# Two units of P times V leave PSUM in one operation; halves out of place move by transfer; a new list of operations

## The chip, the cores and the metric

The kernel runs on one core of a Trainium2 chip. Its time is the device time of one launch in microseconds (us). TensorE (PE) multiplies matrices into PSUM; VectorE (DVE), ScalarE (ACT) and GpSimd (POOL) work element by element; SyncE (SP) and ACT issue transfers, which run on DMA engines beside the rest. Each engine runs its own instructions in the order in which they stand in the program and waits on semaphores for the others.

## The reference, cut to what matters

```
scores = scale * matmul(q, k^T), masked where the clusters of q and k differ     # 4 batches x 8 heads, 768 x 768, head size 64
attn   = exp(scores - max); attn = attn / (sum + 1e-9)
x      = matmul(attn, v), heads side by side                                   # 3072 tokens x 512
h      = x @ w_in;  g = h * tanh(softplus(h))                                  # 512 -> 2048
out    = g @ w_out                                                             # 2048 -> 512
```

## The kernel before

**Units.** The 32 heads (batch b, head h) are cut into three blocks qb of 256 queries: 96 units, in the list `units` in the order head by head, qb 0 1 2. A unit has two halves a of 128 queries. For each half `scores` puts 128 x 768 products into a PSUM buffer of the ring S, which has two buffers; `rowmax` (DVE) takes the row's maximum m, `expo` (ACT) writes p = exp(s - m) to SBUF and the sum l, and with that the buffer of S is free for the scores after next. `total`, `recip`, `p_hi` (POOL) and `p_lo` (DVE) make two fp16 parts hl of the scaled p, and `ptrans` (SP) turns them over by a transposing transfer into pt. The first 24 units (batch 0, the wide ones) keep f32 p and turn it over on PE instead (tiles q, then copies to pt).

**P times V.** `pv(m)` takes the units 2m and 2m+1 together: the first one's product lands on rows 0 to 63 of one PSUM tile o, the second one's on rows 64 to 127, 256 columns each. There is one buffer for o. Unit by unit, `pv_out` (ACT) then writes the high fp16 part of 64 rows to x, and `x_lo` (DVE) the low part as a difference. x is the transposed input of the feed-forward layer, one tile of 128 rows for each pair of heads c = h // 2 and each block qb: even heads own its rows 0 to 63, odd heads its rows 64 to 127, so rows are moved across partitions by these two operations. In the wide units ACT spreads 1/l as rb, DVE multiplies 64 rows a unit into xf, and the odd head's turn ends in one ACT copy and one POOL subtraction of 128 rows.

**Feed-forward.** For batch b and block tt, `m1` multiplies w_in by the four x tiles of tt into the tile h (ring of two), `e_mish` (ACT) applies the activation, `e_gh` (POOL) and `e_gl` (DVE) split it, `m2` multiplies by w_out into O, `m_out` and `m_store` write the rows out. ACT has to load a table each time it goes from exp to Mish and back. The feed-forward of a batch runs among the attention units of the next, and the last 512 tokens use a scheme with fewer products (`n_mul`, `k_mul`) at the end.

**What sets the order.** `ORDER` is a list of operation names written out by hand; `Plan` issues them in its order (an operation that needs another through `pl.after` pulls it forward), and `tie` keeps each engine, and each ring of buffers, in just this order. SP takes 144 transposing transfers and the loads, copies and stores, one after another.

Of the kernel before, what the change touches and what calls it, by code (L numbers as in the profile page):

```python
# [92 lines left out]
def tile_clustered_attention_mish_ffn(  # L93
# [698 lines left out]

    def pv_out(i):
        pl.after(("pv", i // 2, 2), *((("pv_out", i - 1),) if i % 2 else ()))
        g, qb, _ = units[i]
# [8 lines left out]
        if mode(i, 0) != 3:
            nc.scalar.activation(x[r2 : r2 + D, 0], o[:, :256], AF.Copy, scale=1.0 / PS)
            return
        if h % 2 == 0:
            st["xf", h // 2, qb] = hlp.tile([P, 256], F32, tag="hl", name=f"xf{h // 2}_{qb}")
        xf = st["xf", h // 2, qb]
        if i % 2 == 0:  # L810
            st["rb"] = mp.tile([P, 256], F32, tag="osb", name=f"rb{i}", bufs=1)
            nc.scalar.activation(st["rb"], st["o", i // 2][:, 256:], AF.Copy, scale=vst[b, "p"])
        nc.vector.tensor_tensor(xf[r2 : r2 + D], o[:, :256], st["rb"][r : r + D], op=ALU.mult)
        if h % 2:
            nc.scalar.copy(x[:, 0], xf)
            nc.gpsimd.tensor_tensor(x[:, 1], xf, x[:, 0], op=ALU.subtract)

    def x_lo(i):
        pl.after(("pv_out", i))
# [6 lines left out]
        nc.vector.scalar_tensor_tensor(
            x[:, 1], o[:, :256], 1.0 / PS, x[:, 0], op0=ALU.mult, op1=ALU.subtract  # L830
        )
# [732 lines left out]
qk_load 1, qk_load 0, qk_load 2, qk_load 3, v_load 0 3, v_load 0 1, w_load 1, v_load 0 0, w_load 3, v_load 0 2,  # L1564
put_consts, centroids, prep_hi 1, prep_hi 0, prep_lo 0, cent_put, copy_t 1, copy_t 0, v_sq 0 3, copy_a 0, copy_z 0,
prep_lo 1, v_sq 0 1, copy_a 1, w_abs 1, v_sq 0 0, copy_b 0, w_load 2, w_load 0, w_load 16, w_load 7, w_load 4, w_load
17, w_load 6, w_load 11, w_load 5, w_load 10, assign_mm 0, assign_turn 0, assign_max 0, assign_hot 0, assign_back 0,
assign_put 0, hot_direct 1, hot_direct 0, w_abs 3, v_sq 0 2, assign_stg 0, hot_copy 0, scores 0 0, w_low 2, w_low 3,
w_low 1, scores 0 1, rowmax 0 0, rowmax 0 1, w_f32 3, copy_z 1, w_abs 2, hot_copy 1, expo 0 0, expo 0 1, w_abs 0, p_hi
0 1, w_low 0, p_hi 0 0, scores 1 0, p_lo 0 0, scores 1 1, p_lo 0 1, scores 2 0, rowmax 1 0, w_f32 2, v_max 0, rowmax 1  # L1570
1, w_f32 1, w_f32 0, rowmax 2 0, ptrans 0 0, expo 1 0, ptrans 0 1, expo 1 1, p_hi 1 1, p_hi 1 0, p_lo 1 0, scores 2 1,
v_cross 0, p_lo 1 1, ptrans 1 0, copy_b 1, rowmax 2 1, v_peak 0, ptrans 1 1, expo 2 0, w_low 7, prep_hi 2, w_low 6,
prep_lo 2, total 0 1, w_low 17, total 1 1, w_low 5, w_low 4, p_hi 2 0, w_abs 7, expo 2 1, p_hi 2 1, w_sq 0, pv 0 0,
p_lo 2 0, scores 3 0, v_wide 0, scores 3 1, pv 0 1, w_f32 7, recip 0 1, rowmax 3 0, recip 1 1, rowmax 3 1, copy_t 2,
w_load 9, w_load 8, copy_z 2, qk_load 4, hot_copy 2, copy_a 2, w_load 15, copy_b 2, w_load 12, pv 0 2, p_lo 2 1,
scores 4 0, ptrans 2 0, w_abs 5, w_abs 6, w_abs 4, expo 3 0, expo 3 1, ptrans 2 1, p_hi 3 1, p_hi 3 0, p_lo 3 0,
scores 4 1, w_sq 1, p_lo 3 1, scores 5 0, w_f32 6, w_f32 4, v_scale 0, rowmax 4 0, pv_out 0, pv_out 1, rowmax 4 1,
x_lo 0, x_lo 1, ptrans 3 0, expo 4 0, ptrans 3 1, expo 4 1, p_hi 4 1, p_hi 4 0, w_sq 2, p_lo 4 0, w_low 8, w_low 16,
total 3 1, total 4 1, total 2 1, prep_hi 3, prep_lo 3, w_low 9, recip 3 1, rowmax 5 0, recip 4 1, recip 2 1, w_f32 5,
total 1 0, w_abs 8, ptrans 4 0, w_abs 9, expo 5 0, total 0 0, recip 0 0, recip 1 0, scores 5 1, p_lo 4 1, pv 1 0, pv 1  # L1580
1, p_hi 5 0, pv 1 2, w_sq 3, p_lo 5 0, scores 6 0, w_f32 8, rowmax 5 1, ptrans 4 1, w_abs 17, w_f32 17, expo 5 1,
pv_out 2, p_hi 5 1, total 5 1, w_abs 12, recip 5 1, w_abs 16, ptrans 5 0, w_low 12, w_low 10, pv_out 3, w_low 15,
rowmax 6 0, expo 6 0, x_lo 3, scores 6 1, w_sq 4, w_sq 5, w_sq 6, w_sq 7, p_lo 5 1, scores 7 1, w_f32 9, rowmax 6 1,
ptrans 5 1, w_f32 12, rowmax 7 1, expo 6 1, x_lo 2, p_hi 6 1, p_hi 6 0, p_lo 6 0, scores 7 0, pv 2 0, qk_load 5,
qk_load 7, w_load 14, w_load 13, w_load 21, qk_load 6, copy_z 3, copy_t 3, hot_copy 3, w_load 20, copy_b 3, copy_a 3,
w_load 18, w_load 22, w_load 19, v_load 1 0, total 3 0, rowmax 7 0, w_abs 11, w_abs 10, w_abs 14, w_abs 15, w_abs 13,
expo 7 0, ptrans 6 0, expo 7 1, p_hi 7 1, recip 3 0, total 4 0, recip 4 0, total 2 0, recip 2 0, pv 2 1, pv 2 2, w_low
11, w_low 14, w_low 13, total 6 1, total 7 1, w_f32 11, w_f32 14, recip 6 1, w_f32 10, w_f32 13, w_f32 15, w_f32 16,
w_low 21, pv_out 4, p_hi 7 0, assign_mm 1, p_lo 6 1, scores 8 0, w_sq 8, w_sq 9, p_lo 7 0, scores 8 1, w_sq 10, w_sq
11, w_sq 12, p_lo 7 1, w_sq 13, w_sq 14, total 5 0, x_lo 4, assign_turn 1, rowmax 8 0, assign_max 1, recip 7 1, rowmax  # L1590
8 1, ptrans 6 1, w_abs 21, ptrans 7 0, expo 8 0, prep_hi 4, w_f32 21, ptrans 7 1, w_sq 15, expo 8 1, total 8 1, pv_out
5, w_sum 0, p_hi 8 0, p_lo 8 0, scores 9 0, w_spread 0, pv 3 0, p_hi 8 1, assign_hot 1, rowmax 9 0, assign_back 1, pv
3 1, pv 3 2, assign_put 1, scores 9 1, recip 5 0, w_scale 0, recip 8 1, assign_stg 1, rowmax 9 1, w_abs 20, ptrans 8
0, expo 9 0, w_abs 18, pv_out 6, pv_out 7, x_lo 6, x_lo 7, p_hi 9 0, p_lo 8 1, scores 10 0, w_sq 16, p_lo 9 0, ptrans
8 1, expo 9 1, ptrans 9 0, w_low 20, w_low 22, prep_lo 4, w_low 19, w_low 18, w_hi 0, p_hi 9 1, w_f32 18, rowmax 10 0,
w_lo 0, scores 10 1, p_lo 9 1, ptrans 9 1, rowmax 10 1, expo 10 0, expo 10 1, w_abs 19, total 6 0, recip 6 0, w_sq 17,
pv 4 0, total 9 1, w_hi 1, recip 9 1, w_f32 20, w_lo 1, p_hi 10 1, p_hi 10 0, p_lo 10 0, scores 11 0, pv 4 1, pv 4 2,
copy_t 4, copy_a 4, copy_z 4, hot_copy 4, w_load 25, copy_b 4, w_load 26, w_load 23, total 9 0, recip 9 0, scores 11
# [315 lines left out]
```

## Time and profile before

| | us |
|---|---|
| three timed runs | 857.17, 860.67, 860.91 (median 860.67) |
| profiled execution | 856.9, of which the span 855.2 |
| PE busy | 833.8 |
| DVE busy | 675.7 |
| ACT busy | 544.1 |
| POOL busy | 433.6 |

The span runs from the first instruction to the last. Busy shares are averages over stages: up to about 188 us the wide units run, to about 735 us the other units and the feed-forward, then the feed-forward of the last batch alone. Idle time of an engine matters where it is the engine that ends last.

### The profile page before, as it was taken

Reading aid. Unit: us, or ns where it says so; the run is one execution under the profiler, and the core shown is the slowest. Engines: PE = TensorE matmul, PEld = TensorE weight load, DVE = VectorE, ACT = ScalarE, POOL = GpSimd, SP = SyncE. Lnnn points to the kernel's source line nnn. Section 1 sums busy time; section 2 is a strip of 40 time slices with the busy share of each in tenths; the row PEclk is TensorE's granted clock in tenths of the full one; section 3 lists DMA queues with packets and bytes.
Section 4 is the critical chain, followed back from the end, with each engine's and each line's share of the span. In section 5 each row is a group of like instructions: output and inputs, shape, how many; then the busy total and the mean of one; then the engine's idle time right before and its main releaser. Section 6 shows DMA issues by size and latency. Waiting matters only on the chain.

```text
span 855.2 us, 17553 instructions
## 1 busy us (share of the span) xinstructions
PE 833.8 (97%) x6743; PEld 622.9 (73%) x6743; DVE 675.7 (79%) x1192; ACT 544.1 (64%) x925; POOL 433.6 (51%) x417
## 2 busy tenths in 40 slices
PE   8999999999999999999999999999999999999998
PEld 3777776776777677676777766776777776688887
DVE  7899988998788787777878786788878776898822
ACT  7987976775678564676567566576675663455600
POOL 2567865876666465664565356555648433110000
PEclk9999999999999999999999999999999999999999
DMA  9986751798998996986988987888878754000002
GB/s 339 298 247 185 213 135 43 114 192 163 176 200 154 174 181 122 148 163 116 173 153 174 190 171 127 150 177 162 136 146 146 148 112 96 15 1 2 2 8 80
DMA packets 253460, 122.50 MB, mean 143 GB/s; under 512 B 230368, under 2 KB 230880, under 8 KB 253376
## 3 DMA queue, kind: packets, MB, share of 16 engines
q1 hardware_dynamic: 249216, 112.30, 62.7%
q10 hardware_dynamic: 4160, 9.08, 5.3%
q8 instruction: 53, 0.87, 0.4%
q14 instruction: 31, 0.25, 0.1%
HBM read 35.72 MB, written 6.29 MB: 49 GB/s over the span
## 4 chain that ended last, share of the span: by engine, by line
PE 52%; DVE 4%; DMA 3%; ACT 2%; POOL 1%; issue 1%; ACTq 0%; SPq 0%; POOLq 0%; DVEq 0%
PE h L847 7%; PE h L849 6%; PE h L848 6%; PE o L768 5%; PE O L984 5%; PE O L985 5%; PE O L986 5%; PE s L646 3%; PE s L651 3%; DMA pt<-hl 2%; PE cn L937 2%; DVE hl L732 1%; PE cy('k', 1)_10960 L1131 1%; PE cy('k', 0)_10720 L1131 1%; DVE m L663 1%
## 5 line engine op out<-in xcount | busy, mean ns | idle before, releaser
L677 ACT ACTIVATE p<-s,m 128x768 f32<-128x768 f32 x192 | 173.0, 902 | 120.4 <-DVE m L663 59.1
L715 POOL TENSOR_SCALAR hl<-p,l 128x768 f16<-128x768 f32 x144 | 157.3, 1095 | 168.2 <-DVE l L697 92.5
L663 DVE TENSOR_REDUCE m<-s 128x1 f32<-128x768 f32 x192 | 179.8, 949 | 29.5 <-PE s L651 27.1
L732 DVE SCALAR_TENSOR_TENSOR hl<-p,l,hl 128x768 f16<-128x768 f32 x144 | 165.7, 1159 | 30.2 <-POOL hl L715 30.0
L847 PE MATMUL h<-x,w 128*128 128x256 f16 x640 | 175.2, 274 | 0.0
L849 PE MATMUL h<-x,w 128*128 128x256 f16 x640 | 174.5, 273 | 0.0
L848 PE MATMUL h<-x,w 128*128 128x256 f16 x640 | 174.4, 273 | 0.0
L646 PE MATMUL s<-A,B 128*128 128x384 f32 x384 | 117.0, 385 | 11.8 <-ACT p L677 10.0
L984 PE MATMUL O<-w,g 128*128 128x512 f16 x288 | 109.8, 381 | 0.0
L986 PE MATMUL O<-w,g 128*128 128x512 f16 x288 | 109.2, 379 | 0.0
L985 PE MATMUL O<-w,g 128*128 128x512 f16 x288 | 109.2, 379 | 0.0
L651 PE MATMUL s<-Z,T 80*128 80x384 f32 x384 | 99.2, 339 | 0.4 <-DVE T L618 0.4
L847 PEld LDWEIGHTS <-w 128*128 128x128 f16 x768 | 75.1, 98 | 24.4 <-issue 13.2
L864 POOL TENSOR_SCALAR g<-u,mscg 128x512 f16<-128x512 f32 x72 | 70.8, 987 | 43.5 <-ACT u L858 24.9
L848 PEld LDWEIGHTS <-w 128*128 128x128 f16 x768 | 75.3, 98 | 11.3
L646 PEld LDWEIGHTS s<-A,B 128*128 128x128 f32 x384 | 62.0, 190 | 29.2 <-ACT p L677 17.1
L849 PEld LDWEIGHTS <-w 128*128 128x128 f16 x768 | 75.1, 98 | 8.7
L858 ACT ACTIVATE u<-h,msch 128x512 f32<-128x512 f32 x80 | 53.8, 687 | 43.1 <-PE h L849 28.8
L768 PE MATMUL o<-pt,v 128*64 128x256 f16 x1296 | 78.1, 274 | 0.8 <-DMA pt<-hl 0.8
L768 PEld LDWEIGHTS <-v 128*64 128x64 f16 x1296 | 68.1, 110 | 11.8 <-issue 11.3
L872 DVE SCALAR_TENSOR_TENSOR g<-u,mscg,g 128x512 f16<-128x512 f32 x72 | 69.0, 964 | 5.9 <-POOL g L864 5.8
L651 PEld LDWEIGHTS s<-Z,T 80*128 80x128 f32 x384 | 69.9, 189 | 0.7 <-ACT w L285 0.7
(241 smaller groups left out, 1393.2 us busy)
## 6 DMA issues: line engine op xcount, KB each, us to landing
qk<-in_qk_dram SPq DMA_DIRECT2D x32, 384.0 KB, 4.8
stage<-in_w_in_dram SPq DMA_DIRECT2D x16, 512.0 KB, 8.3
stage<-in_w_out_dram SPq DMA_DIRECT2D x16, 512.0 KB, 4.5
vraw<-in_vP_dram SPq DMA_DIRECT2D x16, 384.0 KB, 4.6
Z<-B SPq DMA_DIRECT2D x30, 192.0 KB, 3.4
out_dram<-osb SPq DMA_DIRECT2D x18, 256.0 KB, 3.0
T<-A ACTq DMA_DIRECT2D x23, 192.0 KB, 4.1
B<-T ACTq DMA_DIRECT2D x21, 192.0 KB, 3.9
```

What stands on the lines that cost most here:

```text
L646: nc.tensor.matmul(s[:, j, :384], st["B", n][:, q0 : q0 + P], st["A", n][:, j * 384 : (j + 1) * 384], start=True, stop=False,)
L651: nc.tensor.matmul(s[:, j, :384], st["T", n][: D + NCL, q0 : q0 + P], st["Z", n][: D + NCL, j * 384 : (j + 1) * 384], start=False, stop=True,)
L663: nc.vector.tensor_reduce(m, st["s", i, a][:, :, :384], axis=AX.XY, op=ALU.max, negate=True)
L677: nc.scalar.activation(p.rearrange("p (n x) -> p n x", n=2), st["s", i, a][:, :, :384], AF.Exp, bias=st["m", i, a], scale=1.0, accum_out=l,)
L715: nc.gpsimd.tensor_scalar(t[:, 0], p, r, 1.0, op0=ALU.mult, op1=ALU.mult)
L732: nc.vector.scalar_tensor_tensor(t[:, 1], p, r, t[:, 0], op0=ALU.mult, op1=ALU.subtract)
L768: nc.tensor.matmul(o[s * D : s * D + D, :256], v if early else v[:, int(part == 1)], st["pt", 2 * m + s][:, :, c + (0 if early or part < 2 ...
L847: nc.tensor.matmul(o, wh, xh, start=(c == 0), stop=False)
L848: nc.tensor.matmul(o, wh, xl, start=False, stop=False)
L849: nc.tensor.matmul(o, wl, xh, start=False, stop=(c == 3))
L984: nc.tensor.matmul(o, gh, wh, start=(f == 0 and fi == 0), stop=False)
L985: nc.tensor.matmul(o, gh, wl, start=False, stop=False)
```

## The change

Three pieces of code and the list.

1. The blocks of an even head run in the order 2 1 0, those of an odd head 0 1 2. So of the three tiles o of a pair of heads (k = m % 3) the first holds blocks 2 and 1 of the even head, the second block 0 of both heads, the third blocks 1 and 2 of the odd head.
2. `pv_out` and `x_lo` work once for both units, on 128 rows, row r to row r. The second tile is then in place as a whole. The first goes to the x tile of block 2, where its lower half stands only for the time being; the third goes to a tile xt of its own (a new pool of one buffer).
3. `x_move`, 48 in all, brings the halves that are out of place, 64 rows of 1 KB, to their x tile by a transfer that SP issues. `m1` waits for the moves of its block through `x_ready`.

The tile `idle`, which PE multiplies while it waits at the start, lies in the ring pt now. `ORDER` is a new list with the 48 moves in it; operations of all kinds stand elsewhere in it than before. The core of the diff:

```
-    idle = cp.tile([P, 512], BF16, name="idle")
+    idle = ptp.tile([P, 512], BF16, tag="pt", name="idle")
...
-    units = [(g, qb, g) for g in range(B * H) for qb in range(3)]
+    units = [(g, qb if g % 2 else 2 - qb, g) for g in range(B * H) for qb in range(3)]
...
     def pv_out(i):
         pl.after(("pv", i // 2, 2), *((("pv_out", i - 1),) if i % 2 else ()))
+        if i % 2 == 0:
+            return
+        m = i // 2
...
+        if k == 2:
+            dst = st["xp", m] = xtp.tile([P, 2, 256], F16, tag="xt", name=f"xt{m}")
+        else:
+            dst = st["xp", m] = x_tile(b, c, 2 if k == 0 else 0)
         if mode(i, 0) != 3:
-            nc.scalar.activation(x[r2 : r2 + D, 0], o[:, :256], AF.Copy, scale=1.0 / PS)
+            nc.scalar.activation(dst[:, 0], o[:, :256], AF.Copy, scale=1.0 / PS)
             return
...
-        nc.vector.tensor_tensor(xf[r2 : r2 + D], o[:, :256], st["rb"][r : r + D], op=ALU.mult)
+        nc.vector.tensor_tensor(xf, o[:, :256], rb, op=ALU.mult)
...
+    def x_move(m, s):
+        i = 2 * m + s
+        g, qb, _ = units[i]
+        b, h = divmod(g, H)
+        pl.after(("x_lo", 2 * m + 1))
+        r, r2 = s * D, h % 2 * D
+        if qb == 2:
+            pl.after(("x_move", m - 2, 1))
+        nc.sync.dma_start(x_tile(b, h // 2, qb)[r2 : r2 + D], st["xp", m][r : r + D])
+
+    def x_ready(b, tt):
+        m = [12 * b + 3 * c for c in range(4)]
+        if tt == 0:
+            return [("x_lo", 2 * n + 3) for n in m]
+        return [("x_move", n + 2, tt - 1) for n in m] + [("x_move", n, 1) if tt == 1 else ("x_lo", 2 * n + 1) for n in m]
...
-        pl.after(*(("x_lo", uid[b * H + h, tt]) for h in range(H)), ("moe_scale_h", b), ("w_lo", f))
+        pl.after(*x_ready(b, tt), ("moe_scale_h", b), ("w_lo", f))
...
 ORDER = """
...
+x_lo 74, copy_t 27, m_out 5 1, expo 77 0, pv_out 75, expo 78 1, e_mish 52, copy_a 27, e_mish 53, e_gl 50, x_lo 75, total 77
...
```

How the list moves instructions is shown at three places.

First, DVE at the end of the wide units, before the row maximum m22_0 of unit 22's first half. Names carry the unit and the half (s22_0, m22_0); l are the sums, xf the products of pv_out, w the weights. Before:

```order
L589 STREAM_TRANSPOSE hott2_1949<-hot2_1945 128x768
L365 SCALAR_TENSOR_TENSOR w9_682<-w10_1026,ws1r_1743,w9_682 128x1024
L813 TENSOR_TENSOR xf3_0_1955<-o9_1884,rb18_1956 64x256
L689 TENSOR_SCALAR l20_1890<-l20_1890 128x2
L813 TENSOR_TENSOR xf3_1_1961<-o9_1884,rb18_1956 64x256
L663 TENSOR_REDUCE m22_0_1963<-s22_0_1934 128x1
```

Now:

```order
L366 SCALAR_TENSOR_TENSOR w9_665<-w10_855,ws1r_1756,w9_665 128x1024
L690 TENSOR_SCALAR l20_1893<-l20_1893 128x2
L819 TENSOR_TENSOR xf9_1959<-o9_1897,rb19_1957 128x256
L415 TENSOR_REDUCE vsm1_1963<-vm1_1197 128x1
L664 TENSOR_REDUCE m21_1_1965<-s21_1_1930 128x1
L696 RECIPROCAL l20_1893<-l20_1893 128x2
L664 TENSOR_REDUCE m22_0_1968<-s22_0_1943 128x1
```

Of the two xf operations one is left, and the row maximum m21_1 now stands between it and m22_0, where before it stood further up.

Second, ACT around unit 68 in batch 2, where the squares vq of the next batch's values are taken; vraw is what a load on SP brings. Before:

```order
L860 ACT_TABLE_LOAD
L383 ACTIVATE vq3_1_6752,vm3_6751<-vraw3_1_6743 128x768
L805 ACTIVATE x2_2_1_6234<-o32_6637 64x256
L805 ACTIVATE x2_2_2_6556<-o32_6637 64x256
L677 ACTIVATE p68_0_6756,l68_0_6757<-s68_0_6516,m68_0_6625 128x768
L677 ACTIVATE p68_1_6793,l68_1_6794<-s68_1_6680,m68_1_6764 128x768
```

Now:

```order
L678 ACTIVATE p67_1_6561,l67_1_6562<-s67_1_6454,m67_1_6528 128x768
L384 ACTIVATE vq3_0_6564,vm3_6319<-vraw3_0_6541 128x768
L384 ACTIVATE vq3_3_6566,vm3_6319<-vraw3_3_5555 128x768
L384 ACTIVATE vq3_1_6568,vm3_6319<-vraw3_1_6314 128x768
L678 ACTIVATE p68_0_6718,l68_0_6719<-s68_0_6496,m68_0_6571 128x768
L813 ACTIVATE xt32_6721<-o32_6591 128x256
```

The two x operations have become one, which stands behind p68_0 instead of ahead of it, and three vq stand ahead of p68_0 instead of one.

Third, SP in batch 3, around the transposing transfers of the units 82 and 83. Before:

```order
L748 DMA_TRANSPOSE pt82_8473<-hl82_0_8311 128x12x128
L998 DMA out_0_dram<-osb6_0_8142 128x512
L748 DMA_TRANSPOSE pt82_8473<-hl82_1_8316 128x12x128
L748 DMA_TRANSPOSE pt83_8477<-hl83_1_8456 128x12x128
L529 DMA Z_29_8479<-B_29_8314 64x768
```

Now:

```order
L749 DMA_TRANSPOSE pt82_8427<-hl82_0_8256 128x12x128
L841 DMA x3_1_1_8429<-xx3_7569 64x512
L841 DMA x3_0_1_8431<-xx3_7569 64x512
L841 DMA x3_0_1_8431<-xt38_7957 64x512
L749 DMA_TRANSPOSE pt82_8427<-hl82_1_8251 128x12x128
L841 DMA xx3_7569<-xt38_7957 64x512
L1015 DMA out_0_dram<-osb6_0_8172 128x512
L530 DMA Z_29_8437<-B_29_8403 64x768
L749 DMA_TRANSPOSE pt83_8439<-hl83_1_8406 128x12x128
```

Four moves of the pairs 36, 38 and 39 stand among the transposing transfers of later units; the last of them writes rows that the second one has to have read.

## Rows read from the trace of the kernel before

**Rows 1.** The page: span and PE.

```profile
span 855.2 us, 17553 instructions
PE 833.8 (97%) x6743; PEld 622.9 (73%) x6743; DVE 675.7 (79%) x1192; ACT 544.1 (64%) x925; POOL 433.6 (51%) x417
```

**Rows 2.** Waits of PE, 188 to 740 us: total us, times, longest us.

```profile
PE s L646 <- ACT p L677: 5.6, 6, 1.2
PE s L646 <- issue: 0.9, 1, 0.9
PE o L768 <- DMA pt<-hl: 0.8, 2, 0.4
PE as L558 <- ACT p L677: 0.7, 1, 0.7
```

**Rows 3.** Stretches: length; busy PE, PEld, DVE, ACT, POOL; PEclk, DMA share, GB/s.

```profile
40.00:100.00 60.00, 58.25 (x499) 45.30 (x499) 55.40 (x85) 50.00 (x111) 44.63 (x49) 1.00 0.75 222
100.00:150.00 50.00, 47.16 (x370) 35.53 (x365) 44.03 (x78) 37.10 (x85) 31.10 (x33) 0.97 0.42 105
150.00:188.00 38.00, 36.74 (x296) 28.85 (x296) 35.24 (x63) 27.32 (x45) 29.92 (x27) 1.00 0.82 140
188.00:300.00 112.00, 111.65 (x917) 80.48 (x916) 91.29 (x155) 74.44 (x121) 68.96 (x61) 1.00 0.90 176
```

**Rows 4.** Groups by shape: busy us, mean ns of one, idle before.

```profile
L805 ACT ACTIVATE x<-o 64x256 f16<-64x256 f32 x56 | 21.2, 378 | 24.6 <-PE o L768 19.0 <-PE o L426 3.5 <-PE o L418 1.1
L812 ACT ACTIVATE rb<-o,vsp 128x256 f32<-128x256 f32 x12 | 5.7, 472 | 3.0 <-PE o L780 2.7 <-DVE vsp L406 0.3
L829 DVE SCALAR_TENSOR_TENSOR x<-o,x 64x256 f16<-64x256 f32 x56 | 23.6, 422 | 17.1 <-ACT x L805 12.1 <-ACT xx L805 4.4
L813 DVE TENSOR_TENSOR xf<-o,rb 64x256 f32<-64x256 f32 x24 | 10.0, 419 | 1.0 <-ACT rb L812 0.5
L1139 DVE SCALAR_TENSOR_TENSOR kp<-cy('k', 0)_10720,msco,kt 128x256 f32<-128x256 f32 x1 | 0.5, 485 | 7.4 <-PE cy('k', 0)_10720 L1131 7.4
```

**Rows 5.** The timeline at 138 us and at 31 us: start, us, [idle before].

```profile
135.06 0.96 DVE L663 TENSOR_REDUCE m<-s 128x1 f32<-128x768 f32 x1
137.16 0.62 PE L646 MATMUL s<-A,B 128*128 128x384 f32 x2 [1.55 <-ACT p L677]
138.16 3.51 PE L768 MATMUL o<-pt,vraw 128*64 128x256 f32 x16
30.91 1.95 PE L768 MATMUL o<-pt,vraw 128*64 128x256 f32 x16
```

**Rows 6.** Stretch of the first place, columns as in rows 3.

```profile
138.00:142.00 4.00, 4.00 (x20) 2.06 (x19) 3.94 (x7) 0.91 (x2) 1.67 (x2) 0.57 0.34 68
```

**Rows 7.** The timeline at three waits of PE, 345 to 513 us.

```profile
345.95 0.42 DVE L829 SCALAR_TENSOR_TENSOR x<-o,x 64x256 f16<-64x256 f32 x1 [1.98 <-ACT xx L805]
352.65 0.61 PE L646 MATMUL s<-A,B 128*128 128x384 f32 x2 [0.71 <-ACT p L677]
383.67 0.86 DVE L829 SCALAR_TENSOR_TENSOR x<-o,x 64x256 f16<-64x256 f32 x2 [0.59 <-ACT x L805]
393.27 1.07 PE L558 MATMUL as<-qk,C 128*32 128x512 f32 x8 [0.73 <-ACT p L677]
506.27 0.86 DVE L829 SCALAR_TENSOR_TENSOR x<-o,x 64x256 f16<-64x256 f32 x2 [0.40 <-ACT x L805]
513.05 0.62 PE L646 MATMUL s<-A,B 128*128 128x384 f32 x2 [0.84 <-ACT p L677]
```

**Rows 8.** Timeline of ACT at 493 us and PE behind it.

```profile
493.65 0.84 ACT L383 ACTIVATE vq<-vraw 128x768 bf16<-128x768 f32 x1 [3.25 <-DMA vraw<-in_vP_dram]
496.44 0.61 PE L646 MATMUL s<-A,B 128*128 128x384 f32 x2 [1.20 <-ACT p L677]
```

**Rows 9.** Transfers: SP's issues (ns min/median/max), then sizes and us to landing.

```profile
L529 SPq DMA_DIRECT2D A<-A x12: 467/516/886, 32.3 to 656.4; - x12
Z<-stg SPq DMA_DIRECT2D x30, 48.0 KB, 3.5
```

More of the change, by code (lines that the diff above doesn't have):

```diff
@@ L791, in x_home, with x_tile @@
         return xp.tile([P, 2, 256], F16, tag=f"x{qb}", name=f"x{b}_{c}_{qb}", bufs=T["xbufs"][qb])
+    def x_tile(b, c, qb):
+        if ("x", b, c, qb) not in st:
+            st["x", b, c, qb] = x_home(b, c, qb)
+        return st["x", b, c, qb]
     def pv_out(i):
         pl.after(("pv", i // 2, 2), *((("pv_out", i - 1),) if i % 2 else ()))
+        if i % 2 == 0:
+            return
+        m = i // 2
+        b, h = divmod(units[i][0], H)
+        k, c = m % 3, h // 2
+        o = st["o", m]
+        if k == 2:
+            dst = st["xp", m] = xtp.tile([P, 2, 256], F16, tag="xt", name=f"xt{m}")
+        else:
+            dst = st["xp", m] = x_tile(b, c, 2 if k == 0 else 0)
+        if mode(i, 0) != 3:
+            nc.scalar.activation(dst[:, 0], o[:, :256], AF.Copy, scale=1.0 / PS)
+            return
+        pl.after(("v_scale", b))
+        rb = mp.tile([P, 256], F32, tag="osb", name=f"rb{i}", bufs=1)
+        nc.scalar.activation(rb, o[:, 256:], AF.Copy, scale=vst[b, "p"])
+        xf = hlp.tile([P, 256], F32, tag="hl", name=f"xf{m}")
+        nc.vector.tensor_tensor(xf, o[:, :256], rb, op=ALU.mult)
+        nc.scalar.copy(dst[:, 0], xf)
+        nc.gpsimd.tensor_tensor(dst[:, 1], xf, dst[:, 0], op=ALU.subtract)
@@ L795, in pv_out, with x_lo @@
+    def x_lo(i):
+        pl.after(("pv_out", i))
+        if mode(i, 0) == 3 or i % 2 == 0:
+            return
+        x = st["xp", i // 2]
+        nc.vector.scalar_tensor_tensor(
+            x[:, 1], st["o", i // 2][:, :256], 1.0 / PS, x[:, 0], op0=ALU.mult, op1=ALU.subtract
+        )
+    def x_move(m, s):
+        i = 2 * m + s
         g, qb, _ = units[i]
         b, h = divmod(g, H)
-        if mode(i, 0) == 3:
-            pl.after(("v_scale", b), *((("pv_out", uid[g - 1, qb]),) if h % 2 else ()))
@@ L1323, in tile_clustered_attention_mish_ffn @@
                 pl.at(start(i) + T["pv_out"] if early else i + N["x_lo"] + 0.1 * (u - i), x_lo, u)
+            for k in {0: (1,), 1: (), 2: (0, 1)}[i // 2 % 3]:
+                pl.at(start(i) + T["pv_out"] + 0.3 if early else i + N["x_lo"] + 0.3, x_move, i // 2, k)
     for j in range(80):
@@ L1563 @@
 ORDER = """
[L1564 to L1598, printed above, removed]
@@ new lines @@
+0, rowmax 10 1, expo 10 1, p_hi 10 0, total 10 0, recip 10 0, p_hi 10 1, pv 4 0, scores 11 0, p_lo 10 0, scores 11 1,
+pv 4 1, total 9 1, w_hi 1, w_lo 1, w_f32 20, moe_scale_h 0, rowmax 11 0, recip 8 1, recip 9 1, rowmax 11 1, pv 4 2,
+p_lo 10 1, pv_out 8, x_lo 8, copy_t 4, w_load 18, w_load 25, copy_z 4, v_load 1 1, qk_load 9, hot_copy 4, copy_a 4,
+x_move 2 1, copy_b 4, x_move 2 0, w_load 23, w_load 24, scores 12 0, scores 12 1, w_hi 2, w_low 18, w_abs 25, w_abs
+18, v_sq 1 0, expo 11 0, ptrans 10 0, expo 11 1, p_hi 11 0, total 11 0, recip 11 0, w_f32 18, w_lo 2, w_low 25,
@@ new lines @@
+p_hi 14 1, p_lo 14 0, scores 15 0, rowmax 15 0, rowmax 15 1, pv 6 0, pv 6 1, pv 6 2, p_lo 14 1, pv_out 12, x_lo 12,
+ptrans 14 0, w_abs 28, w_abs 26, w_abs 27, expo 15 0, expo 15 1, ptrans 14 1, p_hi 15 0, total 15 0, recip 15 0, p_hi
+15 1, w_low 27, w_low 28, w_hi 5, total 14 1, w_f32 26, w_f32 28, w_lo 5, w_hi 6, w_f32 27, pv_out 13, w_low 30,
+prep_hi 7, prep_lo 7, w_low 31, x_lo 13, scores 16 0, p_lo 15 0, scores 16 1, w_sq 25, w_sq 26, w_sq 27, p_lo 15 1,
+w_sq 28, scores 17 0, scores 17 1, ptrans 15 0, rowmax 16 0, rowmax 16 1, expo 16 0, expo 16 1, w_lo 6, ptrans 15 1,
@@ new lines @@
+1, scores 20 1, assign_hot 2, ptrans 19 1, rowmax 20 1, recip 19 1, assign_back 2, expo 20 0, expo 20 1, p_hi 20 0,
+total 20 0, recip 20 0, p_hi 20 1, pv 9 0, p_lo 20 0, scores 21 0, pv 9 1, rowmax 21 0, w_lo 9, pv 9 2, pv_out 18,
+x_lo 18, scores 21 1, p_lo 20 1, scores 22 0, ptrans 20 0, expo 21 0, p_hi 21 0, total 21 0, recip 21 0, w_hi 10,
+total 20 1, pv_out 19, v_max 1, rowmax 21 1, recip 20 1, rowmax 22 0, ptrans 20 1, x_lo 19, expo 21 1, p_hi 21 1, p_lo
+21 0, assign_put 2, p_lo 21 1, ptrans 21 0, expo 22 0, p_hi 22 0, total 22 0, recip 22 0, w_lo 10, assign_stg 2,
@@ new lines @@
+19 2, m2 1 0 5, m2 1 0 6, m2 1 0 7, pv_out 38, x_lo 38, scores 43 1, m1 18 0, m1 19 0, scores 42 0, m2 1 1 0, m2 1 1
+1, scores 44 1, m1 19 1, scores 44 0, p_hi 40 1, prep_lo 15, p_hi 40 0, p_hi 41 1, p_lo 40 1, rowmax 42 1, p_lo 40 0,
+rowmax 43 0, p_lo 41 1, ptrans 41 0, qk_load 18, x_move 17 1, copy_z 15, hot_copy 15, ptrans 40 1, ptrans 40 0,
+qk_load 16, ptrans 41 1, v_load 2 2, v_load 2 0, e_mish 16, e_mish 17, pv_out 39, expo 42 1, copy_a 15, m_out 1 0,
+expo 43 0, x_lo 39, total 43 0, recip 43 0, moe_scale_h 1, total 42 1, rowmax 43 1, recip 42 1, rowmax 42 0, expo 42
@@ new lines @@
+22, total 49 0, p_lo 48 0, recip 49 0, recip 49 1, rowmax 50 0, rowmax 50 1, v_spread 2 23, m1 24 0, scores 51 0,
+scores 51 1, m1 24 1, m2 2 1 0, m2 2 1 1, m1 26 0, m1 26 1, scores 52 1, m2 2 1 2, scores 52 0, expo 50 0, expo 50 1,
+pv_out 47, p_hi 49 0, prep_hi 18, prep_lo 18, p_hi 49 1, p_lo 49 0, p_lo 49 1, x_lo 47, v_power 2 23, total 50 1,
+recip 50 1, total 50 0, recip 50 0, rowmax 51 1, rowmax 51 0, e_mish 24, copy_t 18, e_mish 25, expo 51 0, expo 51 1,
+p_hi 50 1, p_hi 50 0, v_high 2 0, v_high 2 1, e_gh 24, p_lo 50 1, p_lo 50 0, rowmax 52 1, total 51 1, total 51 0,
@@ new lines @@
+3 1 3, scores 60 0, pv 28 0, pv 28 1, pv 28 2, m1 36 0, scores 61 0, m2 3 1 4, m2 3 1 5, m2 3 1 6, scores 60 1, m1 36
+1, m2 3 1 7, m1 37 0, m1 37 1, pv_out 56, x_lo 56, scores 62 0, scores 62 1, total 59 1, total 59 0, recip 59 0,
+rowmax 61 1, total 58 1, recip 58 1, e_gl 33, recip 59 1, p_hi 59 0, p_hi 58 1, p_hi 59 1, e_gh 34, e_gh 35, p_lo 58
+1, p_lo 59 0, rowmax 60 0, p_lo 59 1, rowmax 61 0, copy_z 21, hot_copy 21, m_store 3 0, ptrans 58 1, qk_load 24,
+ptrans 59 0, v_load 3 2, ptrans 59 1, copy_a 21, x_move 27 1, expo 61 1, pv_out 57, expo 60 0, expo 61 0, e_mish 36,
```

600 lines of the change are left out of this document (292 added, 308 removed).

## The prediction

> **What bounds the kernel now.** I read the page first, then the waits of PE by stage, then for each wait the timeline of the engine that ended it. PE is busy 833.8 of 855.2 us [rows 1], and the change adds and removes no instruction on PE: the order has 11041 rows on it before and after, the matmuls of each kind in equal numbers. So the time can fall by PE's idle time and by little else: 21.4 us in all. In the middle, 188 to 740 us, PE waits 8.0 us in the four largest groups, and 7.2 of it for the exponential p on ACT or unnamed at the same scores; transposed tiles cost it 0.8 us [rows 2]. In the wide units from 40 to 188 us it stands idle 148 - (58.25 + 47.16 + 36.74) = 5.9 us [rows 3]. The rest lies at the two ends, which the change does not touch. The clock belongs to this too: right behind the longest wait, 1.55 us at 137 us, sixteen matmuls of P times V take 3.51 us against 1.95 us for sixteen at 31 us [rows 5], and the stretch 138 to 142 us shows a granted clock of 0.57 where the others show 1.00 or 0.97 [rows 3, 6]. So a part of it ran at 1.2 instead of 2.4 GHz, and that one wait cost 1.55 + 1.56 = 3.1 us.
>
> ACT and DVE are the engines that are waited for, by queueing: DVE is busy (55.40 + 44.03 + 35.24) / 148 = 91% of the stretch 40 to 188 us [rows 3].
>
> **The change part by part.** *Fewer operations.* In the 72 units that are not wide, 36 of 72 ACT operations and 36 of 72 DVE operations go. The old ones take 0.378 and 0.422 us. 128 rows of 256 columns out of PSUM do not stand in the trace with this output; the nearest are 0.472 us on ACT and 0.485 us on DVE [rows 4], so a pair of units saves between 0.28 and 0.38 us of ACT and between 0.36 and 0.42 us of DVE. I take the lower length on both, since the old row has the same columns, types and operation; ACT falls by 13.6 us (at least 10.2), DVE by 15.2 us (at least 13.0). In the wide units 12 of 24 DVE products of 0.419 us go [rows 4], 5.0 us. All of this lies beside PE's work and is worth nothing but where it stands ahead of an exponential for which PE waits. Those places, one by one:
>
> At 352.65 us PE waits 0.71 us. The DVE operations x and xx run one after another from 345.95 us, and the first itself waited for the second ACT operation [rows 7]. With one of each, what stands behind them on DVE comes 0.38 + 0.43 = 0.8 us earlier, more than the wait; and in the new order both row maxima of unit 50 stand ahead of x on DVE anyway. I count 0.71 us. At 393.27 us (0.73) and 513.05 us (0.84) the chain of waits runs back through such a pair of x operations at 383.67 and 506.27 us, 0.86 us long on DVE and behind two on ACT [rows 7]: again 0.8 us earlier. Sum in the middle: 0.71 + 0.73 + 0.84 = 2.3 us. The bounds are 0, if another queue in the new list is as late, and 8.0 us, if all such waits go. What is late next is POOL's p_hi and the row maximum behind it, which the change leaves as they are. The largest wait of the middle, 1.20 us at 496.44 us, I leave as it is: it stands behind ACT's vq, which waited 3.25 us for a load [rows 8], and of these vq the new order puts three in that place.
>
> At 137 us the row maximum of unit 22 starts at 135.06 us [rows 5], behind two half xf, on DVE. The new order has one whole xf there, but the row maximum of 21_1 as well. PE's order there is the same up to the next scores: six transposes, put2 and six transposes between the scores s22_0 and the first that waits for their buffer. I estimate that m22_0 starts 0.8 us earlier for it; but a second wait, on put2's buffer, comes up behind (DVE has w10 and stg2 to do first), which takes 0.4 back. So the waits fall by 0.4 us, and since neither of the two is as long as 1.55 us, I let the clock stay up: 1.6 us more. Bounds: 0 and 3.1 us. The remaining waits of the wide units are 5.9 - 1.55 = 4.3 us; DVE's share falls from 91 to (134.7 - 5.0) / 148 = 88%, and I take 30% of them, 1.3 us, between 0 and 4.3. Sum for the wide units: 3.3 us.
>
> *The moves.* 48 transfers of 64 KB. The row nearest to them is the on-chip copy of 48 KB, 3.5 us to landing; SP needs 0.52 us to issue one [rows 9], 25 us over the whole kernel. Nothing on PE waits for a move within less than some 20 us: block 0 needs none, and the last two (pair 47) are wanted by m1 80, ahead of which the order has 25 us of matmuls behind the last P times V. On SP each move waits for its x_lo on DVE; in DVE's order each x_lo stands ahead of the hl of the next transposing transfer on SP, so the wait itself holds nothing up. A move into a half that another move empties waits for that one's landing; in the two nearest cases, one of which is shown above, only two or three transfers stand between, and up to 2 us may be lost there. I count 0, because PE's waits on transposed tiles are 0.8 us in all [rows 2]. Without that cover each move costs its issue, 0.52 us.
>
> The Trainium skill's page "DMA: Bandwidth & Descriptors" (Rules for kernel authors) speaks against this part: it advises against transfers of partition halves, since all share the same engines, and says that under 64 KB one pays mostly overhead. No row of before shows what a move of just this shape costs; by that rule the second rival below would weigh more.
>
> *The tile idle* in the ring pt: its last reader runs near the start, ahead of the third pt that would need the buffer. 0. *One buffer for xt*: used by every third pair, emptied by two moves in between. 0.
>
> *The sum.* 2.3 + 3.3 = 5.6 us less than the profiled execution: 856.9 - 5.6 = 851.3 us. That execution lies 3.8 us below the median of the runs shown (860.67), whose lowest is 857.17. Against the median I predict 860.67 - 5.6 = 855.1 us.
>
> **The rivals.** *The waits come back elsewhere.* ORDER is new as a whole; a queue of ACT that is short here is long there. For it: the waits of the middle come from places where ACT is held by something other than x in half of the cases, as at 496.44 us [rows 8], and three vq now stand in one place, two more than before, some 0.9 us each, perhaps with the same 3.25 us of waiting for a load ahead of them. Against it: the change itself takes work from just the two engines that are waited for. Time: 1.9 + 3.25 us at that place cancel the 5.6 us, 860.2 us: no change.
>
> *SP becomes late.* It takes its transfers in order, and a move stands ahead of transposing transfers for which P times V waits. If all 36 moves behind the wide units held one of these up by their issue, PE would wait 36 x 0.52 = 18.7 us, and the time is 860.67 + 18.7 - 5.6 = 873.8 us, slower. It outweighs the gain from 11 of 36 and is measurable as a loss from 20 on. For it: DMA engines are busy to 0.90 from 188 to 300 us [rows 3], so a landing has little room. Against it: two waits of 0.4 us are all that PE has for transposed tiles now.
>
> *All waits of this kind go.* With ACT and DVE shorter and the list fitted to it, PE would lose neither the 8.0 us of the middle nor the 5.9 us and 1.6 us of the wide units: 860.67 - 15.5 = 845.2 us. Against it: the same kind of list with its waits stands in the kernel before.
>
> *The change does not save what it says.* If 128 rows took twice as long as 64, ACT and DVE would gain nothing. The rows of 0.472 and 0.485 us for 128 rows exclude that [rows 4]; I give it 2%.
>
> **How the numbers follow.** The forecast holds 45%, the waits elsewhere 28%, SP 12%, all waits gone 13%, no saving 2%. A difference of 0.5%, 4.3 us, is about what a measurement of this kernel can tell from no change: faster is below 856.4 us, slower above 865.0 us. The forecast's own range is 850.7 to 860.7 (the lower end with some 4 us more of the 8.0 and 5.9 us of waits, the upper with none of the sum), and 0.78 of it is faster. Faster: 0.45 x 0.78 + 0.13 + 0.28 x 0.1 = 0.51. Slower: SP 0.12 x 0.8, a quarter of the waits elsewhere 0.07, and 0.02 from the rest: 0.19. Within: 0.30. The range for 8 in 10 reaches down to the case in which all waits go (846) and up until half of the SP case is left out: 868 us.
>
> **What would show it.** Right: PE's busy time within 1 us of 833.8 and its idle time down to about 16 us; groups of 128 x 256 x<-o with 36 on ACT at 0.38 and 36 on DVE at 0.42 us; no wait of PE over 1 us in the wide units and no clock below 1 in their rows. Wrong: waits of PE on ACT's p of as many us as before (the list), on transposed tiles of several us (SP, or the DMA engines), or a wait of m1 on the moves. My sum would also be wrong if the wide units lose a new stretch to the lower clock.

## The result and the profile after

The changed kernel ("after") takes 846.0 us, median of four runs between 845.35 and 847.34, against 858.9 for four runs of before: a ratio of 0.985, with a 95% interval of 0.982 to 0.988. The forecast was 855.1 us. Its sign was right, and the time lies at the very edge of its range (846), where one rival stood, that all waits of this kind go (845.2 us). Between the medians the time falls by 12.9 us. The profiled execution of after takes 845.51 us, 11.4 less than the 856.9 of before, where the forecast had 5.6 less. The page, for [rows 1]:

```profile
span 843.8 us, 17568 instructions
PE 830.1 (98%) x6742; PEld 625.0 (74%) x6743; DVE 653.7 (77%) x1144; ACT 528.9 (63%) x889; POOL 426.1 (50%) x417
```

PE's idle time fell from 21.4 to 13.7 us, and its busy time, which I had held to be fixed, by 3.7 us. The waits of PE from 188 to 740 us, for [rows 2] (total us, times, longest us):

```profile
PE h L864 <- ACT u L875: 2.3, 1, 2.3
PE s L647 <- ACT p L678: 0.2, 1, 0.2
```

All old waits are gone, and one stands there that before did not have. By stages (columns as in [rows 3]):

```profile
40.00:100.00 60.00, 57.49 (x495) 45.05 (x491) 55.55 (x85) 51.01 (x115) 46.01 (x51) 1.00 0.84 238
100.00:150.00 50.00, 48.64 (x391) 37.57 (x392) 43.82 (x81) 38.15 (x90) 32.17 (x34) 1.00 0.41 113
150.00:188.00 38.00, 37.60 (x329) 30.90 (x325) 35.62 (x54) 28.40 (x43) 33.41 (x26) 1.00 0.87 165
300.00:400.00 100.00, 97.68 (x761) 69.39 (x760) 72.14 (x130) 62.13 (x89) 49.99 (x49) 0.98 0.79 148
400.00:500.00 100.00, 100.00 (x826) 73.07 (x825) 79.15 (x131) 66.35 (x103) 58.95 (x54) 1.00 0.92 179
```

From 40 to 188 us PE stands idle 148 - 143.73 = 4.3 us, 1.6 less than before. The low clock at 138 us is gone: 0.35 us of wait is left where there was 1.55, and the sixteen matmuls behind it take 1.95 us, not 3.51 as in [rows 5]. Timeline of PE in after:

```profile
132.18 0.82 PE L726 MATMUL q<-ident,p 128*128 128x128 f32 x6
132.76 0.59 PE L647 MATMUL s<-A,B 128*128 128x384 f32 x2
...
134.98 0.93 PE L726 MATMUL q<-ident,p 128*128 128x128 f32 x6
136.25 0.62 PE L647 MATMUL s<-A,B 128*128 128x384 f32 x2 [0.35 <-ACT p L678]
...
138.62 1.95 PE L769 MATMUL o<-pt,vraw 128*64 128x256 f32 x16
```

These rows also show what a wait costs. From the start of six transposes to the start of the scores it is 0.58 us without a wait and 1.27 us with one: 0.69 us more, of which the row shows 0.35 as idle. In a full stream the end of one group lies under the start of the next (the scores at 132.76 us start 0.24 us before the transposes end); behind a wait it stands alone and counts as busy. So this wait costs some 0.3 us more than its idle time. For all waits over 20 ns from 10 to 745 us, each set against the usual distance of the same two instructions without a wait, the mean is 0.2 us: 7.0 us for 31 waits of before, 3.6 for 20 of after (three more have no counterpart).

The operations have the lengths that I took from the rows of 64 rows in [rows 4]. Groups by shape of after:

```profile
L813 ACT ACTIVATE x<-o 128x256 f16<-128x256 f32 x16 | 6.1, 382 | 8.6 <-PE o L769 8.4
L828 DVE SCALAR_TENSOR_TENSOR x<-o,x 128x256 f16<-128x256 f32 x16 | 6.7, 421 | 9.4 <-ACT x L813 9.4
L819 DVE TENSOR_TENSOR xf<-o,rb 128x256 f32<-128x256 f32 x12 | 5.0, 420 | 2.9 <-ACT rb L817 2.8
```

128 rows take 0.382 and 0.421 us where 64 rows took 0.378 and 0.422. The moves, beside copies of other sizes ([rows 9]; the last number is us to landing):

```profile
x<-xt SPq DMA_DIRECT2D x24, 64.0 KB, 3.2
Z<-stg SPq DMA_DIRECT2D x30, 48.0 KB, 3.1
Z<-B SPq DMA_DIRECT2D x30, 192.0 KB, 3.7
```

Three times the bytes cost 0.5 us more, so a move's time is mostly fixed. The Trainium skill's page "DMA: Bandwidth & Descriptors" (Rules for kernel authors) says that of transfers under 64 KB; the 3.1 us for 48 KB agree, and a move lies right at that size. PE's waits above show none for a move.

*The new wait.* In the profiled execution PE waits 2.32 us at 368 us for the buffer h, and behind it the clock is low. The timeline of POOL, DVE, ACT and PE in after, each engine waiting for the one shown before it:

```profile
362.77 0.90 POOL L500 TENSOR_SCALAR qk<-qk,scq 128x768 f32<-128x768 f32 x1
363.76 0.83 POOL L503 TENSOR_SCALAR A<-qk 128x768 fp32r<-128x768 f32 x1
364.56 0.69 POOL L881 TENSOR_SCALAR g<-u,mscg 128x512 f16<-128x512 f32 x1
365.22 1.82 POOL L516 TENSOR_TENSOR B<-qk,A 128x768 fp32r<-128x768 f32 x1
...
365.29 2.30 DVE L889 SCALAR_TENSOR_TENSOR g<-u,mscg,g 128x512 f16<-128x512 f32 x1 [3.96 <-POOL g L881]
...
367.70 0.69 ACT L875 ACTIVATE u<-h,msch 128x512 f32<-128x512 f32 x1 [3.14 <-DVE g L889]
...
368.44 0.37 PE L864 MATMUL h<-x,w 128*128 128x256 f16 x1 [2.32 <-ACT u L875]
368.61 0.42 PE L865 MATMUL h<-x,w 128*128 128x256 f16 x1
```

POOL makes qk and A of a later head (`prep_hi 19`) before g (`e_gh 26`), for which DVE, ACT and PE stand in a row. DVE's g takes 2.30 us beside POOL's B. The same matmul waits with this list in the code of before too (newlist_oldcode below: 2.07 us at 376 us), so this wait belongs to the list, not to the shorter operations. The stretch behind (columns as in [rows 3]):

```profile
368.00:372.00 4.00, 3.56 (x18) 2.48 (x18) 3.24 (x7) 3.77 (x5) 0.70 (x1) 0.57 0.81 215
```

### The profile page after: what moved, and what is told of

Its sections match the earlier page's. It is cut to its first block, busy times and chain, and to the rows that moved or that the text cites. A ratio compares the mean times of both kernels' runs of the same rounds, so it can differ in the third digit from the quotient of the medians.

```text
span 843.8 us, 17568 instructions
## 1 busy us (share of the span) xinstructions
PE 830.1 (98%) x6742; PEld 625.0 (74%) x6743; DVE 653.7 (77%) x1144; ACT 528.9 (63%) x889; POOL 426.1 (50%) x417
## 4 chain that ended last, share of the span: by engine, by line
PE 82%; DVE 7%; DMA 4%; ACT 3%; POOL 2%; issue 1%; SPq 0%; ACTq 0%; POOLq 0%; DVEq 0%
PE o L769 11%; PE h L864 9%; PE h L865 9%; PE h L866 9%; PE O L1001 7%; PE O L1002 7%; PE O L1003 7%; PE s L647 7%; PE s L652 6%; DMA pt<-hl 2%; PE cn L954 2%; PE q L726 2%; DVE m L664 1%; ACT p L678 1%; PE as L559 1%
## 5 line engine op out<-in xcount | busy, mean ns | idle before, releaser
L733 DVE SCALAR_TENSOR_TENSOR hl<-p,l,hl 128x768 f16<-128x768 f32 x144 | 172.2, 1207 | 36.4 <-POOL hl L716 35.8
L881 POOL TENSOR_SCALAR g<-u,mscg 128x512 f16<-128x512 f32 x72 | 63.8, 890 | 31.9 <-ACT u L875 20.3
L889 DVE SCALAR_TENSOR_TENSOR g<-u,mscg,g 128x512 f16<-128x512 f32 x72 | 63.6, 888 | 5.6 <-POOL g L881 5.5
```

Of the source, the lines that this page charges most:

```text
L733: nc.vector.scalar_tensor_tensor(t[:, 1], p, r, t[:, 0], op0=ALU.mult, op1=ALU.subtract)
```

## The experiments

Several sessions were run, each with runs of before on the same chip; medians of before were 857.2 to 858.9 us. After itself was timed in two of them: the median of its ten runs is 845.4 us, and differences to after below are against that. Only egh_two_more, egh_no_move and split_act ran beside after; for the others a difference to after goes across sessions, in which before itself moved by up to 1.7 us.

**List or code (three kernels).** *newlist_oldcode* is the code of before with the list of after, without the 48 moves; the two operations of an even unit stand right ahead of those of the odd one. Against the list of after, at one pair:

```
- pv_out 76, x_lo 76, expo 80 1, pv_out 77, copy_b 27, expo 79 1, e_gl 55, x_lo 77, p_lo 79 0,
+ expo 80 1, pv_out 76, pv_out 77, copy_b 27, expo 79 1, e_gl 55, x_lo 76, x_lo 77, p_lo 79 0,
```

> Code of before (two operations of 64 rows a pair of units, moved across partitions by the engine itself, blocks 0 1 2 for all heads, no transfers x_move) with the list of after, from which only the 48 moves are taken out; the even unit's pv_out and x_lo stand right ahead of the odd unit's. Theory A (the shorter queues of ACT and DVE make the gain): about 857 us, as before, between 855 and 860. Theory B (the new list makes it, whatever the code): 846 to 849 us. Theory C (both are needed; the list counts on the short operations): 860 us or more, with new waits of PE on ACT's p behind the x operations.

Measured: 857.79 us, ratio 0.9995 (0.9977 to 1.0014). The list alone gains nothing, as theory A had it. Waits of PE, whole span:

```profile
PE s L646 <- ACT p L677: 3.6, 9, 0.8
PE q L725 <- ACT pt L746: 3.0, 6, 0.9
PE h L847 <- ACT u L858: 2.7, 2, 2.1
```

The waits for p fell from 10.0 us to 3.6, but PE now waits for q (the tiles that ACT and DVE copy away in the wide units) and for h.

*oldlist_newcode* is the other half, the code of after with the list of before and the moves. Against that list, at the same pair:

```
- recip 79 1, e_gl 55, x_lo 77, e_gl 54, m1 57 0,
+ recip 79 1, e_gl 55, x_lo 77, x_move 38 0, x_move 38 1, e_gl 54, m1 57 0,
```

> Code of after with the list of before, into which the 48 moves are put, each right behind the x_lo of the odd unit. Theory A (shorter queues): 850 to 853 us, which is the 5.6 us of my sum or a little more, and the waits of PE at 353, 393 and 513 us gone. Theory B (the list): 857 to 860 us. Theory C (both): 853 to 860 us. If the moves cost anything on SP, waits of PE on transposed tiles of over 2 us show here, since no list was made for them.

Measured: 928.26 us, ratio 1.083 (1.080 to 1.086), far outside all three. The queue of SP in its waits (total us, times, longest us; three of the largest of L841, the moves):

```profile
SPq L841 <- DVE xx L828: 48.0, 6, 12.2
SPq L841 <- DVE xt L828: 40.6, 7, 8.4
SPq L841 <- POOL x L821: 23.3, 4, 9.5
```

With two more groups (21.8 and 18.7 us), SP stands 152 us in front of moves whose data are not ready, with transposes and copies for other units behind them; PE waits 23.9 us for p and 7.1 us for transposed tiles. This is the rival in which SP becomes late, brought about by where the moves stand; 0.52 us a move, as I had priced it, was far too low for that case.

*oldlist_fit* puts the same moves where SP comes to them when their data are there:

```
- ptrans 79 0, ptrans 78 1, ptrans 79 1, ptrans 78 0,
+ ptrans 79 0, ptrans 78 1, x_move 38 0, x_move 38 1, ptrans 79 1, ptrans 78 0,
```

> Code of after, list of before, the 48 moves put into SP's row where by the trace of before their x_lo is done (before the first transfer that started 0.5 us or more behind its end). Theory 1 (the 928 us of the list with moves right behind x_lo came from SP standing in front of moves): 850 to 856 us, SP's waits at the moves under 20 us in all instead of 152. Theory 2 (the old list does not fit the new block order or the later first half, whatever SP does): 870 us or more. If the code's gain needs no new list: 846 to 850 us.

Measured: 864.29 us, ratio 1.006 (1.004 to 1.008): 64 us of the loss were SP's place for the moves, but the result is between the two theories, and the code alone is not faster than before. On the moves' own data SP waits 11 us, not 152 (in front of moves for any reason 23 us, not 176). PE runs the same order as before here, so its waits can be matched one by one. Those at 352.65 and 513.05 us, which I had counted, are gone, and so are 496.44 (1.20 us) and 581.09 (0.87 us), which I had not; the one at 137 us fell from 1.55 to 0.35. The one at 393.27 grew from 0.73 to 1.23, and new ones came, the longest in the wide units (timeline of POOL, then PE; what stopped POOL and what PE waited for stand in the brackets):

```profile
71.32 0.67 POOL L821 TENSOR_TENSOR x<-xf,x 128x256 f16<-128x256 f32 x1 [5.46 <-ACT x L820]
...
79.50 1.80 PE L726 MATMUL q<-ident,p 128*128 128x128 f32 x6 [3.60 <-ACT p L678]
```

POOL's subtraction, which in before waited for an odd head's tile, now comes once for each tile o, and in the old list it stands where its data are not yet there. Ahead of it POOL idles 5.46 us, with work on the weights behind it for which DVE waits, ahead of a row maximum.

The idle time of PE in waits over 20 ns, 10 to 188 and 188 to 745 us, summed from the four traces:

| | list of before | list of after |
|---|---|---|
| code of before | 7.4 + 8.3 (858 us) | 10.0 + 5.2 (857.8 us) |
| code of after | 14.6 + 8.2 (864.3 us) | 5.6 + 2.6 (845.4 us) |

Neither part gains alone; together they take 12 us. So theories A and B both fall, and what theory C says, that both are needed, holds, though not with its times. Each mixed kernel is a single try: the list of before was not fitted further to the code of after, nor that of after to the code of before.

**Long operations cut again.** *split* keeps list, blocks and moves of after:

```
-            nc.scalar.activation(dst[:, 0], o[:, :256], AF.Copy, scale=1.0 / PS)
+            for r in (0, D):
+                nc.scalar.activation(dst[r : r + D, 0], o[r : r + D, :256], AF.Copy, scale=1.0 / PS)
...
```

DVE's xf of the wide units and its x_lo are cut in the same way.

> After, with each operation of 128 rows out of PSUM cut into two of 64 rows (ACT's copy, DVE's difference, DVE's product in the wide units); list, blocks and moves unchanged. It gives ACT 36 x 0.38 = 13.6 us and DVE 48 x 0.42 = 20 us of work back. Theory A: 851 us or more, waits of PE on ACT's p back. Theory B: 846 to 847.5 us. Theory C: like A, 851 us or more.

Measured: 854.52 us, ratio 0.9958 (0.9944 to 0.9973), 9.1 more than after. The number of operations, not the place of the rows, carries 8 to 9 of the 12 us, under this list (8 by the ratios to before of the own session). Waits of PE:

```profile
PE q L726 <- ACT pt L747: 4.1, 9, 0.9
PE h L867 <- ACT u L878: 3.2, 1, 3.2
PE s L647 <- ACT p L678: 2.2, 7, 0.5
```

The same three waits as in newlist_oldcode. Three kernels cut one operation each: *split_wide* the 12 xf, *split_dve* the 36 x_lo, *split_act* the 36 copies.

> After with only the 12 products of DVE in the wide units cut into two of 64 rows (5.0 us of DVE's work given back). In the run with all operations cut, PE lost 4.0 us of busy time between 40 and 188 us, most of it in waits for q, the tiles that ACT and DVE copy to pt. If that comes from these 12 products: 849.5 to 851 us, waits for q of 3 to 4 us. If it comes from ACT's and DVE's operations of the later units: 846 to 847 us. My forecast for these steps was 3.3 us for the wide units.

> After with only DVE's 36 differences x_lo behind the wide units cut into two of 64 rows (15.2 us of DVE's work given back); ACT as in after. My forecast for this and ACT's part was 2.3 us. If DVE's queue carries it: 848 to 850 us, with waits of PE on ACT's p or u behind late row maxima. If ACT's queue carries it: 846 to 847 us.

> After with only ACT's 36 copies behind the wide units cut into two of 64 rows (13.6 us of ACT's work given back). All cuts together cost 8.5 us, the wide products 4.3, DVE's differences 3.0: if the costs add, 847 to 847.5 us; if ACT and DVE stand for each other in one queue (a late copy makes the difference late too), 848.5 to 850 us; if ACT has room, 846 us.

Measured: 850.34 us (ratio 0.9912, 0.9891 to 0.9933), 849.01 us (0.9892, 0.9869 to 0.9914) and 847.01 us (0.9892, 0.986 to 0.9925): 4.9, 3.6 and 1.6 us more than after, together 10.1 against 9.1 for all at once. The costs about add. By the ratio to before of the own session split_dve and split_act stand level, so which of the two costs more is not shown. Waits of PE in split_wide:

```profile
PE q L726 <- ACT pt L747: 4.1, 9, 0.9
```

and in split_dve:

```profile
PE h L865 <- ACT u L876: 3.3, 1, 3.3
PE s L647 <- ACT p L678: 2.7, 7, 0.7
```

Twelve products of 0.42 us on DVE, 5.0 us of work, bring all waits for q back: in the wide units the queue is full, and most of DVE's added work reaches PE. Of the 15.2 us that the 36 differences give DVE back, 2 to 4 reach it; of ACT's 13.6, 1.6 to 2, less than the spread of its runs (845.2 to 850.4).

**The new wait.** *egh_first* changes two names of the list:

```
- prep_hi 19, e_gh 26, prep_lo 19, e_mish 30,
+ e_gh 26, prep_hi 19, prep_lo 19, e_mish 30,
```

> After with one name of the list moved: POOL takes e_gh 26 ahead of prep_hi 19 instead of behind it. In the trace of after PE waits 2.32 us at 368.44 us for m1's buffer h, which ACT frees behind DVE's g, which waits for POOL's; behind it the granted clock shows 3.41 us at 1.2 GHz. If that chain is read rightly: the wait of 2.3 us goes, the clock stays at 1.00 in the stretch 300 to 400 us (1.7 us more), time 842.0 us. If the wait only moves to the units' A, which prep_hi makes: 845.5 to 847 us.

Measured: 842.76 us, ratio 0.9819 (0.9793 to 0.9846), 2.7 less than after and 0.8 above what was expected. PE's waits from 188 to 745 us, and the stretch that had 97.68 us of PE busy at a clock of 0.98:

```profile
PE s L647 <- ACT p L678: 0.5, 1, 0.5
```

```profile
300.00:400.00 100.00, 99.81 (x791) 71.38 (x789) 76.79 (x132) 63.87 (x93) 53.19 (x51) 1.00 0.81 153
```

The chain was read rightly: the wait and the low clock behind it are gone. *egh_two_more* adds two places in the wide units:

```
- w_load 18, w_load 25, copy_z 4, v_load 1 1, qk_load 9, hot_copy 4, copy_a 4, x_move 2 1, copy_b 4,
+ w_load 18, copy_z 4, w_load 25, v_load 1 1, qk_load 9, hot_copy 4, copy_b 4, copy_a 4, x_move 2 1,
...
- rowmax 12 0, w_f32 22, rowmax 12 1,
+ rowmax 12 0, rowmax 12 1, w_f32 22,
```

> egh_first with two more places of the list changed in the wide units. SP: copy_z 4 ahead of w_load 25 and copy_b 4 ahead of copy_a 4 and a move (PE waits 1.09 us for this copy, B<-T, at 79.2 us). DVE: rowmax 12 1 ahead of w_f32 22 (PE waits 0.77 us for p behind this maximum at 85.0 us). If both waits go and stay gone: 840 to 841 us. If they come back in the next units, as the waits of a queue that is full: 842.5 to 843.5 us.

Measured: 842.44 us, ratio 0.9839 (0.9806 to 0.9873): no difference to egh_first that could be told. Both waits went (1.09 and 0.77 us), and others came:

```profile
PE q L726 <- ACT pt L747: 1.5, 4, 0.8
...
PE gram L323 <- DVE w L303: 0.7, 1, 0.7
```

In egh_first these were 0.5 and 0.3 us: of 1.9 us, 1.4 came back at the next places. Both are faster than before and than after: all their runs lie between 841.3 and 844.3 us, all ten of after between 844.4 and 847.3.

**The moves.** *no_move* and *egh_no_move* leave the transfers out of after and of egh_first:

```
-        nc.sync.dma_start(x_tile(b, h // 2, qb)[r2 : r2 + D], st["xp", m][r : r + D])
...
-            dst = st["xp", m] = xtp.tile([P, 2, 256], F16, tag="xt", name=f"xt{m}")
+            dst = st["xp", m] = x_tile(b, c, 1)
```

> After without its 48 moves: the halves out of place stay where the operation of 128 rows put them (the third tile goes straight into the x tile of block 1), so the output holds wrong halves; the list and all other operations are as in after. My sum (moves cost 0): 845 to 847 us. The rival in which SP becomes late, in a small form (each move held something up by its issue of 0.5 to 0.6 us): below 843 us, with PE's waits on DMA and on ACT's p shorter than in after.

> egh_first without the 48 moves (the output holds wrong halves, as in no_move). If the moves cost after its 2.7 us only where they delay POOL's e_gh 26 through a transposing transfer: 842 to 843 us, as egh_first. If each move costs something: 840 us or less.

Measured: 843.27 us (ratio 0.982, 0.9802 to 0.9838) and 844.83 us (0.9863, 0.9833 to 0.9892). Without moves after gains 2.1 us, and egh_first loses 2.1 us. Neither time lies in a range that was expected: no_move is just above that of a small cost (below 843), egh_no_move above both. In no_move the wait at 368 us is missing: SP's transposes start 0.8 to 1.0 us earlier there, and POOL's p_hi comes 4 us earlier (timeline of POOL, after and then no_move):

```profile
355.68 0.91 POOL L716 TENSOR_SCALAR hl<-p,l 128x768 f16<-128x768 f32 x1 [4.65 <-DMA pt<-hl]
351.69 1.68 POOL L716 TENSOR_SCALAR hl<-p,l 128x768 f16<-128x768 f32 x1 [0.67 <-DMA pt<-hl]
```

In egh_no_move there is a new wait at 383 us. Ahead of it POOL idles 6.35 us for a transposing transfer that frees hl, and DVE, ACT and PE follow (waits of PE, 188 to 740 us):

```profile
PE as L559 <- ACT p L678: 2.5, 1, 2.5
```

So taking the moves out is worth 2 us in one order and costs 2 us in the other, and no cost common to both shows. As I read these rows, shifts of 0.5 to 1 us on SP decide whether one wait of 2 to 3 us exists, and it can fall either way.

**After once more.** *after_again* has no edit.

> The kernel after, unchanged, beside the others on the same chip: 845.5 to 847 us. It is there so that differences of 2 to 3 us to egh_first and no_move are read within one session.

Measured: 845.08 us, ratio 0.9867 (0.9837 to 0.9897). Its profile has the same wait at the same place, but another clock (timeline of PE, and the stretch behind it):

```profile
369.25 0.27 PE L864 MATMUL h<-x,w 128*128 128x256 f16 x1 [2.59 <-ACT u L875]
369.36 0.27 PE L865 MATMUL h<-x,w 128*128 128x256 f16 x1
```

```profile
369.00:373.00 4.00, 3.75 (x32) 3.29 (x32) 3.26 (x8) 3.76 (x5) 0.89 (x2) 1.00 0.86 210
```

## Why the prediction was right, and where it was not

By terms, from the two profiled executions:

| | forecast | measured |
|---|---|---|
| waits of PE, 188 to 740 us | -2.3 | -5.7 (8.3 to 2.6) |
| waits of PE, 40 to 188 us | -1.7 | -1.6 (5.9 to 4.3) |
| clock at 138 us | -1.6 | -1.6 |
| clock at 368 us | not counted | about +1.6 |
| moves, `idle`, `xt` | 0 | 0 |
| what a wait costs beyond its idle time (estimate) | not counted | about -3.4 |
| sum | -5.6 | -11.4 in all |

The forecast of 855.1 us started from a median of three runs, 860.67 us, which a fourth run brought to 858.9; the fall of 5.6 us has to be set beside 11.4 us in the profiles and 12.9 in the medians. So the range held by its edge, and that the time lies close to the rival's 845.2 us is chance: the rival had all 15.5 us of waits and clock gone, but 6.9 us of waits stayed; the cost of a wait beyond its idle time, which it left out, and the high median that it started from made up for them.

*The middle* is the term that was mis-sized: I counted the three waits whose chain ran back through a pair of x operations, 2.3 us, and left the rest. All of the 8.0 us of [rows 2] went. The runs show why the count by places could not find that. With the old list the shorter operations did remove two of my three waits, but just as much came up elsewhere (8.3 to 8.2 us); with the new list alone the waits fell to 5.2; only together to 2.6. I read it as one queue with more or less room in it, not as a set of separate places. The argument from single places had the right sign but does not stand as the cause: its own test, oldlist_fit, was slower than before. My objection to the rival in which all such waits go, that before had such a list too, counted for nothing; that the old list had been made for longer queues fits the table, but no run shows it by itself.

*The new wait at 368 us* is what I had given to the rival of waits that come back, at another place. It stands in seven profiles with this list (after, after_again, the four split kernels and newlist_oldcode: 1.8 to 3.3 us) and is gone only where POOL's two operations change places or the moves are left out of the code of after. The three vq that I feared cost nothing: they stand there one behind the other without a wait for the load, the first at 476.70 us, then (ACT, after):

```profile
477.65 0.84 ACT L384 ACTIVATE vq<-vraw 128x768 bf16<-128x768 f32 x1
...
478.62 0.84 ACT L384 ACTIVATE vq<-vraw 128x768 bf16<-128x768 f32 x1
```

*PE's busy time* was to stay within 1 us of 833.8, and the time to fall "by PE's idle time and by little else". That step failed: busy fell by 3.7 us. It did not fit my own sum either, in which the 1.6 us of the clock are busy time. Between 10 and 745 us PE has 32 waits over 20 ns in before and 22 in after (scores that start behind a wait show 0.44 us of their own busy time, the others 0.18); what these waits cost beyond their idle time came to 7.0 and 3.6 us above, 3.4 us less. With that estimate the terms come to 10.7 of 11.4 us; the remaining 0.7 are not assigned.

*The wide units* came out as forecast in size, but by luck in the parts: at 137 us the waits fell by 1.0 us (1.55 to 0.24 and 0.35), where I had 0.4, and the others by 0.6, where I had 1.3. That DVE was the engine, split_wide (4.9 us for 12 products, against 3.3 for all steps there) shows. The prices of the operations, 0.38 and 0.42 us, were right, as was the choice of the lower bound. *The moves* at 0 came out for this list, within the 2 us that the runs without moves leave open; how far they lean on the list is shown by 928 us. No wait over 1 us was to be left in the wide units; one is, 1.23 us at 80 us for a copy (B<-T).

*The clock* was to stay up in the wide units, and did in both profiles of after. But the price that I gave it belongs to an execution, not to the kernel (below).
